# A ConvNeXt-V2 block on one core: x turned by DMA transposes while loading, the convolution as 32x32 tiles, one chunk of three evacuated by VectorE

## The chip, the core and the metric

The kernel runs on one core of a Trainium2 chip. The core has TensorE (PE, with its weight loads listed apart as PEld), VectorE (DVE), ScalarE (ACT), GpSimd (POOL), SyncE (SP, which here only issues DMAs) and 16 DMA engines. The metric is the device time of one execution in microseconds; lower is better.

## The reference, cut to what matters

```python
# x: (1, 512, 512, 96) bf16, dw: (3, 3, 96), w1: (96, 384), w2: (384, 96)
out = sum over i, j of  xp[:, i:i+H, j:j+W, :] * dw[i, j]     # depthwise 3x3, zero padding of 1
h = layernorm(out, over channels, eps=1e-5)
h = gelu(h @ w1)                                              # tanh form, 384 channels
gx = sqrt(sum of h*h over all pixels + 1e-6)                  # one number per channel
nx = gx / (mean of gx over channels + 1e-6)
h = grn_gamma * (h * nx) + grn_beta + h
return x + h @ w2
```

The sum of squares over all 512 x 512 pixels divides the kernel into two passes: no output can be made before every pixel has been through the Gelu.

## The kernel before, in words

**Blocks.** The image is cut into 128 blocks of four rows (GR = 4), 2,048 pixels each. A pixel's 96 channels are handled as three chunks of 32. The tile that comes out of the convolution has 128 partitions = 4 groups x 32 channels and, for each of the three chunks, 512 columns of pixels.

**First pass, slot by slot.** A loop over slots `s` writes all engines' work in one fixed order (the wrapper InOrder keeps the program's order on each engine, and for that reason nearly all instructions have the line of the wrapper, L35). In a slot of the steady stage stand together: the load of x for block s + 4 (`load_x`, on SP), the convolution of block s (`conv_taps`, three bursts of matmuls, `conv(0)` to `conv(2)`, and then `evac`), the layer norm of the blocks before (sums by matmuls with `rowsel`, 1/std on GpSimd, broadcast by way of DRAM into `rbc`, product `yn` on GpSimd), the writing of `yn` to DRAM and reading back as `ynT` with channels on the partitions, and for a block some slots back the first matrix and the Gelu (`mlp_units`: units of one or two PSUM banks, 12 banks in all; `unit(0, 2)` is the first, with the matmuls `PS<-ynT,w1p` and the Gelu `g<-PS`). Sums of squares of `g` come partly from BN_STATS on VectorE (`entry`, called by `squares(0)` to `squares(2)` for the first two quads of a block and by `squares_rest` for the others) and partly from matmuls of `g` with itself (`gram_next`). The order of a steady slot is:

```python
conv(0); unit(0, 2); unit(2, 1); squares(0)
conv(1, False); spread_out()
turn_x(s + 3)
unit(3, 1); unit(4, 2); squares(1); gram_next(1)
unit(6, 1); squares(2); unit(7, 1)
stage_turn(k)              # one slot in four: VectorE turns 1/std
conv(2); evac(); gram_next(1)
unit(8, 2); unit(10, 1); stage_stats(b2); unit(11, 1); squares_rest(2)
```

A `pe.drain()` follows the bursts where `fence` is true. In the steady slots the convolution always accumulates into the same three PSUM banks, `Y3`, so burst 0 of a block must wait until `evac` has read the block before.

**x, before.** `load_x` brings four rows as 128 partitions of 16 pixels, with one pixel of overlap at each side (18 pixels, 3,456 bytes per partition), into one of four `xin` buffers. `turn_x` turns it on VectorE in 32x32 blocks with two instructions per block (the first 64 channels as pairs of 32-bit words) into a ring of five `xT` tiles, where the partitions are 4 rows x 32 channels. A matmul of the convolution reads 64 partitions, that is two rows, and writes 32, one output row, so that up to two vertical taps are one matmul with the weights `Wq`: 8 tiles of the array (2 x 4), three shifts dx, three chunks, 72 matmuls per block, 24 in each burst. A row outside of the image is read from `zrow`, a tile of zeros.

**evac, before.** ScalarE copies all three banks to `y_bf` (128x1536) in bf16.

**The last 14 blocks** pass the first matrix after the last convolution (`mlp_tail`), and **the second pass** multiplies by `W2s`, adds x and the bias (`xb`, GpSimd) on VectorE (`o_sb`) and stores; parts of `g` are kept or reloaded, the rest is made again from `ynT` (`gr`).

Of the kernel before, what the change touches and what calls it, by code (L numbers as in the profile page):

```python
# [8 lines left out]
ALU = mybir.AluOpType  # L9
ACTF = mybir.ActivationFunctionType  # L10
AX = mybir.AxisListType

GR = 4
# [43 lines left out]
def kernel(  # L57
# [11 lines left out]
    f32 = mybir.dt.float32  # L69
    i32 = mybir.dt.int32  # L70
    bf16 = x.dtype
# [38 lines left out]
    def chans(i):  # L110
        return slice(i, 64, 2) if i < 2 else slice(64, 96)
# [4 lines left out]
    def quad(flat_ap, t):  # L116
        return flat_ap.rearrange("p r (t g m) -> p t g r m", t=NQ, m=MB)[:, t]

    def quad_out(flat_ap):
        return flat_ap.rearrange("p (g r m) -> p g r m", r=GR, m=MB)  # L120
# [20 lines left out]
    Wq = consts.tile([128, NI, 3, GR, 32], bf16, name="Wq")  # L141
# [41 lines left out]
    SL = PXP + 2  # L183
    with ExitStack() as p1:
# [25 lines left out]
        xinpool = pc.enter_context(tc.tile_pool(name="xin", side="right", bufs=4))  # L210
        xins = {}

        def shift(h, j):
            return 1 if (h, j) == (0, GR - 1) else -1 if (h, j) == (1, 0) else 0

        def load_x(b):
            t = xinpool.tile([128, SL, C], bf16, name="xin")
            off = x.offset + b * GR * W * C
            rows = lambda p0, p1, s0, s1: (
                t[p0:p1, s0:s1, :].rearrange("p g c -> p (g c)"),  # L220
                bass.AP(x.tensor, off + (p0 * PXP - 1 + s0) * C, [[PXP * C, p1 - p0], [1, (s1 - s0) * C]]))
            if b == 0:
                pool.memset(t[0:1, 0, :], 0.0)
                parts = [(16, 128, 0, SL), (0, 16, 1, SL), (1, 16, 0, 1)]
            elif b == NBLK - 1:
                pool.memset(t[96:128, SL - 1, :], 0.0)
                parts = [(0, 112, 0, SL), (112, 128, 0, SL - 1), (112, 127, SL - 1, SL)]
            else:
                parts = [(0, 128, 0, SL)]
            for part in parts:  # L230
                o, i_ = rows(*part)
                sp.dma_start(out=o, in_=i_)
            xins[b] = t

        Wd = gpool.tile([128, NQ, NCH, QW], bf16, name="g")[:].rearrange("p t j w -> p (t j w)")[
            :, :NI * 9 * 32].rearrange("p (i k c) -> p i k c", i=NI, k=9)
# [5 lines left out]
        for b in range(min(2, NBLK)):  # L242
            load_x(b)
        act.activation(out=warm[:], in_=warm[:], func=ACTF.Gelu_apprx_tanh)
        act.activation(out=Wq[:].rearrange("p i d j c -> p (i d j c)").rearrange("p (a w) -> p a w", a=3),
                       in_=zrow[:, None, :NI * GR * 32].to_broadcast([128, 3, NI * GR * 32]), func=ACTF.Identity)
# [8 lines left out]
        xtpool = pc.enter_context(tc.tile_pool(name="xt", side="right", bufs=1))  # L255
# [6 lines left out]
        NXT = 5  # L262
        xt_ring = []
        xt_all = xtpool.tile([128, NXT, NI, SL * MB], bf16, name="xT")
        for i in range(NXT):
            xt_ring.append(xt_all[:, i])
        assert NXT * NI * SL * MB >= NQ * NCH * QW
        g_over = xt_all[:].rearrange("p x i s -> p (x i s)")[:, :NQ * NCH * QW].rearrange(
            "p (t j w) -> p t j w", t=NQ, j=NCH)
# [32 lines left out]
        def cm_unit(g, ynt, t):  # L302
            U = banks3()
            for j in range(NCH):
                pe.matmul(quad_out(U[:, j, :]), lhsT=w1p[:, j * 128:(j + 1) * 128],
                          rhs=quad(ynt[:], t), start=True, stop=True)
            act.activation(out=g[:, t, :, :], in_=U, func=ACTF.Gelu_apprx_tanh)

        def px_unit(g, ynt, t):
            Uf = banks3().rearrange("p k w -> p (k w)")  # L310
            for r in range(GR):
                c = r * E
                while c < (r + 1) * E:
                    sz = min((r + 1) * E - c, W - c % W)
                    pe.matmul(Uf[:, c:c + sz], lhsT=ynt[:, r, t * 128:t * 128 + 128],
                              rhs=w1p[:, c - r * E:c - r * E + sz], start=True, stop=True)
                    c += sz
            act.activation(out=g[:, t, :, :].rearrange("p j w -> p (j w)"), in_=Uf, func=ACTF.Gelu_apprx_tanh)
# [9 lines left out]
        def stage_mm2(n, q):  # L328
            g, xb = grp[q]["g"], grp[q]["xb"]
            GQ = QW // 128  # L330
            o_sb = late.o.tile([128, PXP, C], bf16, name="o_sb")
            for sub in range(NSUB):
                O = out_bank()
                for gl_ in range(GPS):
                    gg = sub * GPS + gl_
                    for j in range(NCH):
# [3 lines left out]
                dve.tensor_tensor(out=o_sb[:, sub * GPS:(sub + 1) * GPS, :], in0=O,  # L340
                                   in1=xb[:, sub * GPS:(sub + 1) * GPS, :], op=ALU.add)
# [57 lines left out]
        n = 0  # L399
        for h in range(2):  # L400
            for j in range(GR):
                for q in (2 * h, 2 * h + 1):
                    a = q + GR * shift(h, j) - j + 1
                    if 0 <= a < 3:
                        n += 1
                        o, i_ = Wq[32 * q:32 * q + 32, :, :, j, :], Wd[32 * q:32 * q + 32, :, 3 * a:3 * a + 3, :]
                        if n % 2:
                            act.activation(out=o, in_=i_, func=ACTF.Identity)
                        elif n % 4:
                            dve.tensor_copy(out=o, in_=i_)  # L410
                        else:
                            pool.tensor_copy(out=o, in_=i_)

# [28 lines left out]
        def turn_x(b):  # L442
            xin = xins.pop(b)
            t = xt_ring[b % NXT]
            pairs = t[:, 0:2, :].rearrange("p i s -> p (i s)").bitcast(f32)
            dve.transpose(out=pairs.rearrange("p (g m) -> p g m", m=MB),
                          in_=xin[:, :, 0:64].bitcast(f32))
            dve.transpose(out=t[:, 2, :].rearrange("p (g m) -> p g m", m=MB), in_=xin[:, :, 64:96])

        def x_rows(b, p0, p1, i, c0, n):  # L450
            t = xt_ring[b % NXT]
            if i == 2:
                return t[p0:p1, 2, c0:c0 + n]
            return t[p0:p1, 0:2, :].rearrange("p i s -> p (i s)").rearrange(
                "p (s e) -> p s e", e=2)[:, c0:c0 + n, i]

# [6 lines left out]
        def conv_taps(b, spare):  # L463
# [6 lines left out]
            for n in range(3):  # L470
                mms.append([(h, j, (n + h) % NI, dx) for dx in (0, -1, 1) for j in range(GR) for h in range(2)])
            flat = [m for ms in mms for m in ms]
            first = {}
            last = {}
            for n, (h, j, i, dx) in enumerate(flat):
                first.setdefault((i, j), n)
                last[i, j] = n

            def burst(n, fence=True):
                k = sum(len(ms) for ms in mms[:n])  # L480
                for h, j, i, dx in mms[n]:
                    src = b + shift(h, j)
                    o0, o1 = max(0, -dx), W - max(0, dx)
                    pe.matmul(
                        Y[i][32 * j:32 * j + 32, o0:o1],
                        lhsT=Wq[64 * h:64 * h + 64, i, dx + 1, j, :],
                        rhs=x_rows(src, 64 * h, 64 * h + 64, i, MB * (1 + dx) + o0, o1 - o0)
                        if 0 <= src < NBLK else zrow[64 * h:64 * h + 64, o0:o1],
                        start=first[i, j] == k,
                        stop=last[i, j] == k,  # L490
                    )
                    k += 1
                if n < 2 and fence:
                    pe.drain()

            def evac():
                y = ypool.tile([128, NI, W], bf16, name="y_bf")
                if spare:
                    act.activation(out=y[:, 0:2, :], in_=Ua, func=ACTF.Identity)
                    act.activation(out=y[:, 2, :], in_=Ub[:, 0, :], func=ACTF.Identity)  # L500
                else:
                    act.activation(out=y[:], in_=Y3, func=ACTF.Identity)
                ybf[b] = y
# [195 lines left out]
        def mlp_units(b):  # L699
# [5 lines left out]
            def cm_mm(dst, j, t):  # L705
                pe.matmul(quad_out(dst), lhsT=w1p[:, j * 128:(j + 1) * 128], rhs=quad(yt[:], t), start=True, stop=True)

            def unit(bank, n):
# [10 lines left out]
                while c < end:  # L719
# [4 lines left out]
                    else:  # L724
# [3 lines left out]
                        col = (cm_quads(b) + t) * 128  # L728
                        pe.matmul(Uf[:, c - c0:c - c0 + sz], lhsT=yt[:, r, col:col + 128], rhs=w1p[:, e0:e0 + sz],
# [93 lines left out]
        turn_x(0)  # L823
        turn_x(1)
        turn_x(2)
        for s in range(last_slot + 1):
# [34 lines left out]
            elif not mlp:  # L861
                if s + 3 < NBLK:
                    turn_x(s + 3)
# [21 lines left out]
            else:  # L885
# [10 lines left out]
                if s + 3 < NBLK:  # L896
                    turn_x(s + 3)
# [100 lines left out]
    with p2:  # L998
        def out_part(q, o_sb, sub):
# [3 lines left out]
                    "(p g) c -> p g c", g=PXP)[:, sub * GPS:(sub + 1) * GPS],  # L1003
                in_=o_sb[:, sub * GPS:(sub + 1) * GPS])
# [47 lines left out]
```

## Time and profile before

| | |
|---|---|
| median of 3 runs | 1489.95 us (1483.42 to 1490.06) |
| profiled execution, its own time | 1482.67 us |
| its span in the trace | 1480.8 us |
| granted TensorE clock, mean | 0.994 |
| DMA | 433.08 MB, 292 GB/s on average |
| first pass with convolution | to about 885 us |
| second pass | from about 1,020 us |

In the profile a row of a group reads: line, engine, operation, out<-in by the program's names, partitions and elements with their types, number of instructions, then busy time in us, mean ns of one, and the idle time of the engine before them with what ended it. In the timeline a row reads: start in us, length in us, engine, line, operation, and how many instructions were merged into the row. In the table by windows each engine's busy us is followed by its number of instructions; then come the granted clock, the share of the 16 DMA engines that was busy, and GB/s. Ends of matmuls are modelled, so that TensorE looks fuller than it is. An instruction of ScalarE or VectorE can begin before the one ahead of it has left the pipeline, so that the distance between starts is shorter than the mean length.

### The profile page before, as it was taken

To read this page: it belongs to the slowest core of one execution; us is meant where nothing else is said; L and a number is where in the kernel's file an instruction comes from. 1 tells how busy PE (TensorE), PEld (TensorE's weight loads), DVE (VectorE), ACT (ScalarE), POOL (GpSimd) and SP (SyncE) were. 2 spreads that over 40 slices of the span, in tenths; PEclk is the share of its full clock that TensorE was granted. 3 is DMA by queue.
4 is the path that set the end of the run, shared out by engine and by line. 5 is a ranking of instruction groups with operands and counts; after the bars stand their busy time and mean duration, and the time that the engine had idled before them with its cause. 6 is when DMAs were issued, how large, how long until landed. Compare 5 with 4: busy or idle time off the path is not lost.

```text
span 1480.8 us, 54225 instructions
## 1 busy us (share of the span) xinstructions
PE 1391.3 (94%) x23125; PEld 810.4 (55%) x23125; DVE 1182.0 (80%) x2135; ACT 1414.4 (96%) x1595; POOL 1300.3 (88%) x922
## 2 busy tenths in 40 slices
PE   8888999999999999999999997789999999999998
PEld 3434444444444444444444445467777777776776
DVE  7849989999999999999999987965555555555555
ACT  7888989999999999999999999999999999999997
POOL 3459889998998999998999987569999999999997
PEclk9999999999999999999999999999999999999999
DMA  5568788788888888888888866669999999999997
GB/s 180 179 205 255 241 253 280 228 271 260 260 248 264 258 264 255 276 253 254 263 258 266 263 216 195 195 225 409 366 359 402 417 416 413 419 410 417 411 412 282
DMA packets 167768, 433.08 MB, mean 292 GB/s; under 512 B 31558, under 2 KB 81318, under 8 KB 163046
## 3 DMA queue, kind: packets, MB, share of 16 engines
q1 hardware_dynamic: 151284, 326.04, 66.3%
q0 software_dynamic: 14880, 103.43, 17.6%
q8 instruction: 181, 2.97, 0.8%
q14 instruction: 61, 0.50, 0.1%
q10 hardware_dynamic: 1362, 0.15, 0.1%
HBM read 273.30 MB, written 156.22 MB: 290 GB/s over the span
## 4 chain that ended last, share of the span: by engine, by line
PE 30%; ACT 24%; DMA 19%; POOL 13%; DVE 6%; issue 4%; SPq 4%; POOLq 0%; ACTq 0%; DVEq 0%
PE PS L35 30%; ACT g L35 16%; DMA out_dram<-o_sb 9%; POOL yn L35 6%; ACT y_bf L35 5%; POOL ysq L35 5%; SPq L35 4%; DMA yn_dram<-yn 3%; DVE bst L35 3%; DMA xin<-in_x_dram 2%; DMA rbc<-r_dram 2%; DMA ynT<-yn_dram 1%; DMA g_dram<-g 1%; DVE o_sb L35 1%; ACT xT L35 1%
## 5 line engine op out<-in xcount | busy, mean ns | idle before, releaser
L35 ACT ACTIVATE g<-PS 128x512 bf16<-128x512 f32 (+2 forms) x1062 | 727.7, 864 | 16.5 <-PE PS L35 15.6
L35 DVE BATCH_NORM_STATS2 bst<-g 128x6 f32<-128x512 bf16 x1110 | 671.3, 672 | 35.4 <-ACT g L35 34.5
L35 PE MATMUL PS<-ynT,w1p 128*128 128x512 bf16 x2181 | 609.6, 381 | 23.6 <-ACT g L35 5.4
L35 ACT ACTIVATE gr<-PS 128x1536 bf16<-128x1536 f32 x360 | 498.5, 1459 | 18.8 <-PE PS L35 13.8
L35 POOL TENSOR_TENSOR yn<-y_bf,rbc 128x1536 bf16<-128x1536 bf16 x126 | 391.3, 3108 | 77.3 <-ACT rbc L35 21.9
L35 DVE TENSOR_TENSOR o_sb<-PS,xb 128x384 bf16<-128x384 f32 x512 | 277.3, 556 | 227.0 <-PE PS L35 190.1
L324 POOL TENSOR_TENSOR xb<-xr,B2c 128x1536 f32<-128x1536 bf16 x118 | 368.1, 3133 | 4.3 <-DVE o_sb L35 2.0
L35 PE MATMUL PS<-xT,Wq 64*32 64x511 bf16 (+1 forms) x9198 | 340.5, 389 | 26.2 <-ACT y_bf L35 8.1
L35 POOL TENSOR_TENSOR ysq<-y_bf 128x1536 bf16<-128x1536 bf16 x114 | 313.6, 2752 | 12.8 <-ACT y_bf L35 12.8
L35 PEld LDWEIGHTS <-w1p 128*128 128x128 bf16 x2181 | 171.6, 98 | 222.0 <-issue 133.4
L35 PEld LDWEIGHTS <-gr 128*128 128x128 bf16 x4296 | 212.1, 98 | 68.9 <-issue 12.0
L35 PE MATMUL PS<-W2s,gr 128*128 128x96 bf16 x4224 | 223.5, 206 | 8.2 <-DVE o_sb L35 8.0
L35 PEld LDWEIGHTS <-Wq 64*32 64x32 bf16 x9216 | 111.9, 90 | 193.3 <-issue 145.9
L35 ACT ACTIVATE y_bf<-PS 128x1536 bf16<-128x1536 f32 (+2 forms) x135 | 199.4, 1482 | 17.4 <-PE PS L35 13.3
L35 DVE STREAM_TRANSPOSE xT<-xin 128x576 f32<-128x576 f32 (+1 forms) x256 | 181.4, 748 | 8.1 <-DMA xin<-in_x_dram 8.1
L35 PEld LDWEIGHTS <-g 128*128 128x128 bf16 x1704 | 104.9, 98 | 86.3 <-issue 54.3
L35 PE MATMUL PS<-w1p,ynT 128*128 128x256 bf16 (+2 forms) x822 | 125.8, 273 | 8.0 <-ACT xT L35 3.2
L35 PE MATMUL PS<-g 128*128 128x128 bf16 x1464 | 122.6, 220 | 2.9 <-DVE PS L35 2.6
L35 PEld LDWEIGHTS <-gl 128*128 128x128 bf16 x1680 | 82.8, 98 | 26.8 <-issue 5.0
L35 PE MATMUL PS<-W2s,gl 128*128 128x96 bf16 x1680 | 89.5, 206 | 3.4 <-DVE o_sb L35 3.2
L35 PEld LDWEIGHTS <-ynT 128*128 128x128 bf16 x822 | 64.1, 97 | 31.5 <-issue 13.7
L279 POOL DMA_DIRECT2D xr<-in_x_dram x115 | 63.7, 555 | 14.2 <-POOL xb L324 14.2
(105 smaller groups left out, 576.5 us busy)
## 6 DMA issues: line engine op xcount, KB each, us to landing
xin<-in_x_dram SPq DMA_DIRECT2D x126, 432.0 KB
g_dram<-g SPq DMA_DIRECT2D x105, 512.0 KB
gl<-g_dram POOLq DMA_DIRECT2D x35, 1536.0 KB, 11.3
yn_dram<-yn SPq DMA_DIRECT2D x512, 96.0 KB
ynT<-yn_dram SPq DMA_DIRECT2D x128, 384.0 KB
out_dram<-o_sb SPq DMA_DIRECT2D x127, 384.0 KB
xr<-in_x_dram POOLq DMA_DIRECT2D x123, 384.0 KB, 6.9
ynT<-yn_dram SPq DMA_DIRECT2D x85, 512.0 KB
```

The costliest lines, as they stand in the source:

```text
L35: r = f(*a, **k)
L279: pq.dma_start(out=xr[:], in_=x[0, r0:r0 + GR].rearrange("r w c -> (r w) c").rearrange("(p g) c -> p g c", g=PXP))
L324: pq.tensor_tensor(out=xb[:], in0=grp[q]["xr"][:], in1=bias[:, None, :].to_broadcast([128, PXP, C]), op=ALU.add)
```

## The change

- **Load.** `load_x` issues one DMA per block with `transpose=True`: the block's 196,608 elements, seen as 128 rows of 1,536, arrive turned, with no overlap at the sides. A partition is now one of 128 = 4 x 32 places in a run of 16 pixels x 96 channels: pixel modulo four and chunk are mixed as 3 x pixel + chunk. The ring holds six blocks in one tile `xT` (NXT = 6). `turn_x` and `xin` are gone.
- **Convolution.** The weights are `Wd`, diagonal 32x32 blocks for each chunk and tap; the copies into `Wq` are gone. A matmul reads 32 partitions and writes the 32 of one pixel of four (`sx`). A burst has one dx and runs over dy, chunk and sx. Where sx + dx leaves the four pixels, the matmul covers 384 of the 512 columns and a second one, right behind it and with the same weights, covers the remaining 124. Where the rows needed cross the end of the ring, a round is cut in two. Matmuls per block: 36 for dx = 0 and 45 for each of the other two, and more where it is cut.
- **evac.** ScalarE takes chunks 0 and 1, VectorE chunk 2.
- **Order of pixels.** With the new order of columns, `quad` is a plain slice, `quad_out` is gone, and the second pass writes and reads `o_sb` and `xb` with a step of four pixels.

```diff
 def chans(i):
-    return slice(i, 64, 2) if i < 2 else slice(64, 96)
+    return slice(32 * i, 32 * i + 32)
 def quad(flat_ap, t):
-    return flat_ap.rearrange("p r (t g m) -> p t g r m", t=NQ, m=MB)[:, t]
+    return flat_ap[:, t, :]
-Wq = consts.tile([128, NI, 3, GR, 32], bf16, name="Wq")
+Wd = consts.tile([128, NI, 9, 32], bf16, name="Wd")
...
-xinpool = pc.enter_context(tc.tile_pool(name="xin", side="right", bufs=4))
+NXT = 6
+xt = xtpool.tile([128, GR, NI, NXT * 128], bf16, name="xT")
 def load_x(b):
...
+    c = b % NXT * 128
+    sp.dma_start(out=xt[:, :, :, c:c + 128].rearrange("p k a s -> p (k a) s"),
+                 in_=x[0, b * GR:(b + 1) * GR].rearrange("r w c -> (r w c)").rearrange(
+                     "(p e) -> p e", p=128), transpose=True)
...
-    for n in range(3):
-        mms.append([(h, j, (n + h) % NI, dx) for dx in (0, -1, 1) for j in range(GR) for h in range(2)])
+    for dx in (0, -1, 1):
+        mm = []
+        for dy in (0, -1, 1):
+            runs = ...                       # rows of the ring: one run, or two where it wraps
+            for r, at_, nr in runs:
+                o = slice(r * MB, (r + nr) * MB)
+                for i in range(NI):
+                    for sx in range(GR):
+                        wrap = not 0 <= sx + dx < GR
+                        q = NI * ((sx + dx) % GR) + i
+                        ko, ki = slice(0, GR), slice(0, GR)
+                        if wrap:
+                            ko, ki = (slice(1, GR), slice(0, GR - 1)) if dx < 0 else (
+                                slice(0, GR - 1), slice(1, GR))
+                        yo = Y[i][32 * sx:32 * sx + 32, :].rearrange("p (k s) -> p k s", k=GR)
+                        xi = xt[32 * (q % 4):32 * (q % 4) + 32, :, q // 4, :]
+                        w = Wd[32 * (q % 4):32 * (q % 4) + 32, i, 3 * (dy + 1) + dx + 1, :]
+                        mm.append(((i, sx), w, yo[:, ko, o], xi[:, ki, at_:at_ + nr * MB]))
+                        if wrap:
...
+                            mm.append(...)   # the remaining columns, same weights
+        mms.append(mm)
...
 def evac():
-    act.activation(out=y[:], in_=Y3, func=ACTF.Identity)
+    act.activation(out=y[:, 0:2, :], in_=Y3[:, 0:2, :], func=ACTF.Identity)
+    dve.tensor_copy(out=y[:, 2, :], in_=Y3[:, 2, :])
...
-    turn_x(s + 3)
...
 # second pass
-dve.tensor_tensor(out=o_sb[:, sub * GPS:(sub + 1) * GPS, :], in0=O,
-                  in1=xb[:, sub * GPS:(sub + 1) * GPS, :], op=ALU.add)
+dve.tensor_tensor(out=o_sb[:, sub::NQ, :], in0=O, in1=xb[:, sub::NQ, :], op=ALU.add)
```

## The prediction

> **What bounds the kernel now.** I read the totals first, then the windows table of single blocks, then the timeline of one block, then the groups by form for durations. Over the span no engine is alone:
>
> ```profile
> PE 1391.3 (94%) x23125; PEld 810.4 (55%) x23125; DVE 1182.0 (80%) x2135; ACT 1414.4 (96%) x1595; POOL 1300.3 (88%) x922
> ```
>
> The change touches the stage in which a block is convolved while an earlier one goes through the first matrix and Gelu: 114 blocks, about 90 to 885 us. The 128 evacuations of the convolution (y_bf) follow each other there every 7.03 us. The windows table of one such block (busy us and count of PE, PEld, DVE, ACT, POOL, then clock, DMA share, GB/s):
>
> ```profile
> core 0: us, PE busy (x) PEld busy (x) DVE busy (x) ACT busy (x) POOL busy (x), PEclk, DMA share, GB/s
> 550.95:557.98 7.03, 6.78 (x120) 3.15 (x120) 7.03 (x12) 7.03 (x11) 7.03 (x3) 1.00 0.80 261
> ```
>
> Everything looks full, so busy shares don't decide. The timeline of the same block does:
>
> ```profile
> 549.36 1.58 ACT L35 ACTIVATE y_bf<-PS 128x1536 bf16<-128x1536 f32 x1
> ...
> 550.69 5.93 ACT L35 ACTIVATE g<-PS 128x1024 bf16<-128x1024 f32 x9
> ...
> 550.99 0.89 PE L35 MATMUL PS<-xT,Wq 64*32 64x512 bf16 x24
> 551.32 5.40 DVE L35 BATCH_NORM_STATS2 bst<-g 128x6 f32<-128x512 bf16 x9
> ...
> 552.00 0.82 PE L35 MATMUL PS<-ynT,w1p 128*128 128x512 bf16 x3
> ...
> 556.37 1.60 ACT L35 ACTIVATE y_bf<-PS 128x1536 bf16<-128x1536 f32 x1
> 556.64 1.42 DVE L35 STREAM_TRANSPOSE xT<-xin 128x576 f32<-128x576 f32 x2
> ...
> 558.02 0.43 PE L35 MATMUL PS<-xT,Wq 64*32 64x512 bf16 x8
> ```
>
> The convolution has one set of three PSUM banks (Y3). So there is a ring: y_bf ends (549.36 + 1.58 = 550.94), burst 0 of the next convolution starts 0.05 later, and 1.22 us after that the second matmul of unit(0,2) starts; 0.46 later ScalarE starts its Gelu, and from there ScalarE runs without a gap through six Gelus and y_bf, 5.30 us. 0.05 + 1.22 + 0.46 + 5.30 = 7.03, the period, in nearly every block. It ends again at 556.37 + 1.60 = 557.97, and TensorE starts at 558.02.
>
> What slack have the others? TensorE: I set each distance between starts against the smallest of its kind, 300 to 800 us. 17 us of excess over 71 blocks, 0.24 per block, nearly all of it before burst 0; so TensorE needs 6.79. VectorE: nine BN_STATS at 0.59 start to start, 5.3, two transposes 1.4, and small ones: nothing to spare, but not in the ring. GpSimd needs 6.5.
>
> **The change part by part.** Rows by form for the costs:
>
> ```profile
> L35 DVE TENSOR_TENSOR o_sb<-PS,xb 128x384 bf16<-128x384 f32 x512 | 277.3, 556 | 227.0 <-PE PS L35 190.1 <-DMA out_dram<-o_sb 35.4 <-POOL xb L324 0.9
> L35 ACT ACTIVATE y_bf<-PS 128x1024 bf16<-128x1024 f32 x7 | 7.2, 1022 | 7.3 <-PE PS L35 7.3
> L35 DVE TENSOR_SCALAR mom<-PS 128x128 f32<-128x128 f32 x31 | 8.5, 275 | 3.3 <-PE PS L35 3.3
> L35 DVE MEMSET PS<- 128x128 f32 x34 | 5.6, 165 | 3.4
> ```
>
> *ScalarE's evacuation* shrinks from three banks (1.57) to two: 1.02 to 1.10 at the end of a queue. ScalarE's ring: 7.03 - 1.57 + 1.10 = 6.56.
>
> *VectorE's evacuation* is new, 128x512 f32 from PSUM, which no row shows. The two rows that read PSUM give (556 - 275) / 256 = 1.10 ns a column, so 0.70; the 128x512 MEMSET of PSUM (2.44 us into the span) took 0.485, so below 0.45 is unlikely. I take 0.65, nearer the readers. Where it stands matters more: in VectorE's program it follows the block's six BN_STATS of the first two quads, and the first pair of these reads the Gelu of unit(0,2). And burst 0's ninth matmul (the first of chunk 2) waits for it. So there is a second ring: 0.05 + 1.23 + 0.46, that Gelu in full 1.08, 0.03 to VectorE (30 waits for Gelu ended so), 6 x 0.59 = 3.54, copy 0.65, 0.05 = 7.09; less 0.03 for the eight matmuls that go ahead; in one slot of four VectorE's rstd transpose (0.23) stands in between, 0.06 on average. **7.12**, with the copy's bounds 6.92 to 7.17. That is the wait that takes the place of the one removed, and it is as long.
>
> *VectorE's transposes* go: 256, 1.42 per block. They weren't in the first ring, and are not in the second. VectorE then needs 5.3 + 0.65 + about 0.15 = 6.1 per block and idles before the first pair.
>
> *The matmuls.* 72 per block (64 rows, 8 tiles at once, three rounds per burst) become 36 + 45 + 45, on 32 rows, 12 different tiles at once: again three rounds per burst. A round takes 0.23 (starts at 501.754, .987, 502.214). Weight load and matmul of free tiles start 3.4 ns apart, so 12 fill in 0.04 instead of 0.03. In bursts 1 and 2 three tiles of twelve take two matmuls per round, 384 and 124 columns, 0.25 instead of 0.23, or 0.27 if the short one waits for its 90 ns weight load. Per block +0.11 to +0.19; where the ring of six wraps (one block of three) a round is split in two, up to +0.12 more. TensorE: 6.90 to 7.10. It fits into the 0.24 that TensorE waited, so it is not in the sum, but it leaves no cover.
>
> That holds only if a tile that waits doesn't hold back the matmuls behind it. The last block shows it, where matmul 7 of each round of eight reads zrow:
>
> ```profile
> 878.34 0.41 PE L35 MATMUL PS<-xT,Wq 64*32 64x512 bf16 x6
> 878.36 0.39 PE L35 MATMUL PS<-zrow,Wq 64*32 64x512 bf16 x1
> 878.36 0.60 PE L35 MATMUL PS<-xT,Wq 64*32 64x512 bf16 x3
> 878.58 0.38 PE L35 MATMUL PS<-zrow,Wq 64*32 64x511 bf16 x1
> 878.59 0.60 PE L35 MATMUL PS<-xT,Wq 64*32 64x511 bf16 x6
> 878.80 0.38 PE L35 MATMUL PS<-zrow,Wq 64*32 64x511 bf16 x1
> ```
>
> Round 1: seventh, as written. Round 2: third. Round 3: second. Each starts when its own tile is free. The Trainium skill (TensorE: Matmul & The Clock Gate, Part 3: Packing small matmuls — row/col tiling) says that matmuls start and end strictly in program order; by that the second rival below would be the forecast. The rows speak against it, though only by some 20 ns of overtaking.
>
> *The loads.* Before, a block's 432 KB took 128 packets of 3,456 B at 172 ns, 1.37 us of 16 engines. A transposed 384 KB is in no row. Lower bound: 96 pieces of 4,096 B at 199 ns, 1.2. Upper: 12,288 writes of 32 B at the 10.6 ns of the 64 B packets, 8.1. In between, the source is read in runs of 256 B, 1,536 of them; between 64 B (10.6 ns) and 1,024 B (56) that is 20 ns, 1.9 us. I take 1.9, as the source runs are whole. The rest of the block's DMA is 0.82 x 7.03 - 1.37 = 4.4 us, so 6.3 of 7.1. It stays hidden below 2.7. The Trainium skill (DMA: Bandwidth & Descriptors, Latency and other measured facts) gives a transposing DMA 261 GB/s, an estimate of 1.5 us; the sum would be the same.
>
> SP issues as many DMAs as before (0.57 each for x; SP is busy 71%). The load of block s+4 now waits for the convolution of block s-1 instead of VectorE. Set against the trace, half of the loads were issued before that, by up to 5 us. Queued behind on SP are the reads of ynT and the writes of yn and rbc, used a slot or more later, and x itself was issued some 25 us before its use. 0 to 0.1 us per block; I take 0.
>
> *Setup and ramp.* The nine Wq copies go (2.5 us), but TensorE's fill matmuls run until 8.1 us anyway. In the ramp 1.4 us of transposes stood before yn (18.36 to 19.79), and the copy of 0.65 comes in. -6 to 0; I take -3. The second half has strided o_sb and the last block's four stores in runs of 192 B: below 1 us.
>
> **Sum.** Against the profiled execution's own time, 1482.67 (span 1480.8 plus 1.9; 0.5% under the median 1489.95 of the three runs, and like the fastest, 1483.42): 114 x (7.12 - 7.03) = +10, -3: **1490**. Its own range: 6.92 to 7.27 per block and -6 to 0, so 1464 to 1510.
>
> **The rivals.**
> - *Faster.* The copy takes 0.45 and TensorE's extra is 0.11: both rings at 6.9, (6.90 - 7.03) x 114 = -15, -3: 1465. For it: ScalarE's 6.56 and VectorE's 6.1 both leave room. Against: TensorE at 6.90 is then the floor, so no more than this.
> - *Tiles in order* (slower). If the 124-column matmul holds back the queue until its tile's 384 columns have passed, bursts 1 and 2 become chains of nine steps: 0.162 (a 384-column matmul to the next), 0.014 as between rounds, 4 starts of 3.4 ns: 0.19 each, 1.71 in place of 0.46 and at the tail a little less, +2.3 per block. TensorE needs 9.1: +236, and 14 slots without Gelu 32 more: 1750. It decides as soon as the extra is over 0.35.
> - *Transposing loads too slow* (slower). Over 2.7 us a block the 16 engines are the bound: at 3.5 the block takes 7.9, +100, 1580; at the upper bound 12.5, 2100. For it: DMA share is 0.80 already. Against: the loads are one large piece each, and far ahead.
>
> **How the numbers follow.** The second ring, 1490: 0.50. Faster, 1465: 0.20. Tiles in order: 0.10. Loads: 0.20, of which 0.12 below 1640. The range goes from 1460 to 1640 and leaves out the tiles in order and the worse loads, 0.18. About 0.5%, 7.4 us, is what a measurement here can tell from no change. The forecast straddles that: of its 0.50, 0.05 faster, 0.20 the same, 0.25 slower. Faster 0.25, same 0.20, slower 0.55.
>
> **What would show it.** Right: y_bf on ScalarE near 1.1 and on VectorE near 0.65, ScalarE idle some 0.5 us per block before the Gelu of unit(0,2), VectorE idle before its first pair, and burst 0 released by VectorE's y_bf. Wrong: convolution bursts over 1.1 us each (order), waits for xT or a DMA share near 1 (loads), or a period under 6.9, which would mean that VectorE's pairs start earlier than the ring says.

## The result, and the profile after

The changed kernel takes 1571.93 us (median of 4, 1565.07 to 1577.23), where the kernel before took 1490.0 on the same chip: 1.056 times as long, 95% interval 1.051 to 1.061. That lies in the forecast range, on the side named as likeliest, but 82 us above the time forecast. The profiled execution took 1570.23, with a span of 1568.5.

Where the time went is read from the evacuations of the convolution (y_bf), one per block. The table gives their times from the two traces; "ramp" is the start of the 18th, "steady" the 110 blocks from there to the 128th, "rest" all after that.

| us | ramp | steady | rest | mean period | median period |
|---|---|---|---|---|---|
| before | 99.1 | 784.6 | 597.1 | 7.13 | 7.04 |
| after | 121.6 | 850.8 | 596.0 | 7.74 | 7.29 |

What follows the 128th evacuation, nearly all of it the second pass, takes what it took. The first pass loses 22.5 in the ramp and 66 in the steady stage. The totals of the page (busy us, share of the span, instructions):

```profile
PE 1439.7 (92%) x31801; PEld 926.0 (59%) x31801; DVE 1102.2 (70%) x2004; ACT 1372.6 (88%) x1581; POOL 1296.5 (83%) x917
```

VectorE and ScalarE have more room, and TensorE has 8,700 pairs of weight load and matmul more. The new groups by form (busy us, mean ns | idle before them, what ended it), and the durations of SP's issue of a load (shortest, median, longest ns):

```profile
L35 PE MATMUL PS<-xT,Wd 32*32 32x384 bf16 x3360 | 253.4, 336 | 12.4 <-issue 10.8
L35 PE MATMUL PS<-xT,Wd 32*32 32x124 bf16 x2040 | 170.4, 220 | 2.5 <-issue 2.5
...
L35 ACT ACTIVATE y_bf<-PS 128x1024 bf16<-128x1024 f32 x128 | 135.9, 1062 | 55.5 <-PE PS L35 55.0 <-POOL nt L35 0.3
L35 DVE CAST y_bf<-PS 128x512 bf16<-128x512 f32 x128 | 86.0, 672 | 53.4 <-PE PS L35 53.1
```

```profile
L35 SPq DMA_TRANSPOSE xT<-in_x_dram x128: 1356/2084/3003, 0.7 to 935.3; - x128
```

An undisturbed block is a little shorter than before. The windows table (columns in its first line) and the timeline (start, length, what, idle before it) of one block:

```profile
core 0: us, PE busy (x) PEld busy (x) DVE busy (x) ACT busy (x) POOL busy (x), PEclk, DMA share, GB/s
610.98:617.90 6.92, 6.83 (x177) 3.81 (x177) 5.99 (x11) 6.66 (x11) 4.91 (x2) 1.00 0.95 226
```

```profile
610.43 0.68 DVE L35 CAST y_bf<-PS 128x512 bf16<-128x512 f32 x1
...
610.98 1.01 PE L35 MATMUL PS<-xT,Wd 32*32 32x512 bf16 x36
...
612.77 3.90 ACT L35 ACTIVATE g<-PS 128x1024 bf16<-128x1024 f32 x6 [0.26 <-ACT g L35]
612.83 0.89 PE L35 MATMUL PS<-xT,Wd 32*32 32x384 bf16 x45
...
613.83 3.66 DVE L35 BATCH_NORM_STATS2 bst<-g 128x6 f32<-128x512 bf16 x6 [0.93 <-ACT g L35]
...
616.50 1.08 ACT L35 ACTIVATE y_bf<-PS 128x1024 bf16<-128x1024 f32 x1
...
617.40 0.67 DVE L35 CAST y_bf<-PS 128x512 bf16<-128x512 f32 x1
...
617.89 0.41 PE L35 MATMUL PS<-xT,Wd 32*32 32x512 bf16 x8
```

This is the ring by way of VectorE: ScalarE idles 0.26 before the Gelu of unit(0, 2), VectorE idles 0.93 before its first pair, and the ninth matmul of the next convolution waits for VectorE's copy. From the end of one copy to the end of the next: 1.66 to the Gelu, 1.06 to the first pair, 3.57 to the copy, 0.67 the copy, 6.96. Only 47 of the 110 periods are below 7.15, though; before there were 104. What the engines wait for between 300 and 900 us (total, times, longest):

```profile
DVE bst L35 <- ACT g L35: 89.4, 78, 3.1
ACT g L35 <- PE PS L35: 36.2, 48, 2.5
POOL yn L35 <- DMA rbc<-r_dram: 35.1, 10, 4.9
PE PS L35 <- issue: 26.4, 34, 1.9
...
PE PS L35 <- DVE y_bf L35: 12.4, 8, 3.0
```

Two of these are new in kind. GpSimd waits 35 us for `rbc`, a DMA, against 6.6 before. And TensorE waits 26 us for nothing that the profile shows ("issue"); before it did not at all in that window. The DMA queues of the same 600 us (packets, MB, share of 16 engines' time), first before, then after:

```profile
q1 hardware_dynamic: 78931, 151.89, 80.9%
q8 instruction: 80, 1.31, 1.0%
```

```profile
q1 hardware_dynamic: 183274, 138.46, 99.2%
q8 instruction: 115, 1.88, 1.3%
```

Fewer bytes (a load is 384 KB instead of 432, and the 600 us hold fewer blocks), and the engines are full. The queue of instructions carries nearly half as much again in packets of 16 KB: TensorE's longer program. One of TensorE's waits, in the timeline of its instructions:

```profile
664.40 0.88 PE L35 MATMUL PS<-xT,Wd 32*32 32x384 bf16 x44
667.21 0.37 PE L35 MATMUL PS<-xT,Wd 32*32 32x512 bf16 x1 [1.94 <-issue]
```

It stops one matmul short of the end of a burst, whose inputs and banks are all there, and goes on 1.27 after the end of a packet of instructions. There are 46 such stops of over 0.4 us in the first pass, 48 us together; each ends 1.2 to 1.7 us after a packet (median 1.39, where a random moment lies 2.7 after one). The kernel before has one.

The clock differs as well. The two ramps in the windows table (columns as above), first before, then after:

```profile
0.00:99.14 99.14, 84.75 (x1833) 37.72 (x1834) 68.63 (x167) 77.62 (x91) 45.16 (x57) 0.98 0.60 180
0.00:121.63 121.63, 99.66 (x3014) 58.65 (x3015) 53.55 (x142) 67.07 (x77) 43.78 (x53) 0.83 0.71 150
```

The granted clock of TensorE is 0.98 on average in the ramp before and 0.83 after; it is at 0.5 for 3.4 and 41 us. In the steady stage it is 0.99 in both. At most, (1 - 0.83) x 121.6 = 21 us of the ramp after go to the clock (an estimate), against 2 before.

### The profile page after: what moved, and what is told of

Read it like the earlier page. It is cut to its first block, busy times and chain, and to the rows that moved or that the text cites. A ratio compares the mean times of both kernels' runs of the same rounds, so it can differ in the third digit from the quotient of the medians.

```text
span 1568.5 us, 71465 instructions
## 1 busy us (share of the span) xinstructions
PE 1439.7 (92%) x31801; PEld 926.0 (59%) x31801; DVE 1102.2 (70%) x2004; ACT 1372.6 (88%) x1581; POOL 1296.5 (83%) x917
## 5 line engine op out<-in xcount | busy, mean ns | idle before, releaser
L35 DVE BATCH_NORM_STATS2 bst<-g 128x6 f32<-128x512 bf16 x1110 | 680.7, 677 | 149.1 <-ACT g L35 147.6
L35 PE MATMUL PS<-xT,Wd 32*32 32x512 bf16 (+1 forms) x17892 | 394.5, 341 | 58.3 <-issue 33.7
L35 PEld LDWEIGHTS <-Wd 32*32 32x32 bf16 x17892 | 225.6, 90 | 235.0 <-issue 209.3
L35 ACT ACTIVATE y_bf<-PS 128x1024 bf16<-128x1024 f32 x128 | 135.9, 1062 | 55.5 <-PE PS L35 55.0
L35 DVE CAST y_bf<-PS 128x512 bf16<-128x512 f32 x128 | 86.0, 672 | 53.4 <-PE PS L35 53.1
```

What stands on the lines that cost most here:

```text
L35: r = f(*a, **k)
```

## The experiments

Theory A: the turned loads fill the DMA engines, `rbc` and `ynT` come late, and all else follows. Theory B: the load of block s + 4 waits on SP for the convolution of block s - 1, because the ring has six places, and holds up what is queued behind it. Theory C: TensorE's longer program isn't fetched in time. Theory D: the copy on VectorE passes delays on to the next convolution. All in one table; "stops" are those of TensorE as above, from 10 to 970 us; "DMA" is the sum of packet times from the 25th to the 127th evacuation over 16 engines (packets that overlap can bring it above 1); "period" is the mean from the 18th.

| | median us | ratio, 95% interval | pairs | stops, us | DMA | period |
|---|---|---|---|---|---|---|
| before | | 1 | 23,125 | 1, 1.6 | 0.82 | 7.13 |
| after | 1571.93 | 1.056 (1.051 to 1.061) | 31,801 | 46, 48.2 | 1.00 | 7.74 |
| e1_plain_load | 1533.86 | 1.036 (1.032 to 1.040) | 31,489 | 30, 30.8 | 0.87 | 7.46 |
| e2_half_load | 1526.61 | 1.033 (1.027 to 1.039) | 31,489 | 31, 28.7 | 0.92 | 7.39 |
| e3_ring8 | 1562.83 | 1.056 (1.051 to 1.062) | 30,996 | 33, 43.7 | 0.99 | 7.66 |
| e4_evac_scalar | 1562.55 | 1.055 (1.051 to 1.059) | 31,489 | 48, 49.7 | 1.00 | 7.65 |
| e5_before_split | 1542.62 | 1.044 (1.039 to 1.049) | 32,341 | 32, 32.1 | 0.80 | 7.40 |
| e6_before_extra | 1539.37 | 1.040 (1.036 to 1.045) | 23,125 | 2, 1.2 | 1.03 | 7.54 |
| e7_plain_lean | 1503.38 | 1.017 (1.013 to 1.022) | 27,460 | 6, 9.3 | 0.90 | 7.21 |
| e8_after_lean | 1546.97 | 1.041 (1.038 to 1.045) | 27,460 | 7, 8.5 | 1.00 | 7.59 |
| e9_split_one | 1489.40 | 1.004 (1.001 to 1.007) | 26,197 | 6, 8.3 | 0.83 | 7.17 |
| e10_split_extra | 1610.29 | 1.086 (1.081 to 1.092) | 32,341 | 81, 91.9 | 1.00 | 8.13 |
| e11_lean_no_load | 1493.85 | 1.005 (1.003 to 1.008) | 27,460 | 7, 8.8 | 0.67 | 7.15 |
| e12_short_aggr | 1475.35 | 0.998 (0.997 to 1.000) | 27,733 | 9, 9.2 | 0.67 | 7.00 |

Each ratio is to the kernel before on the same chip (1476.94 to 1490.0). Pairs are those that the trace recorded, of which about one in a hundred is missing (after, e1, e2 and e4 have the same program for TensorE, and so have e7, e8, e11 and e12).

**The loads and the ring of six.**

e1_plain_load:

```diff
-             "(p e) -> p e", p=128), transpose=True)
+             "(p k s) -> p k s", p=128, s=128))
```

> The changed kernel with the same 128 loads into the same places, but as plain copies without turning (x is not turned, so the convolution's numbers are meaningless; all else is as in the changed kernel, the runs of 256 B too). Theory A (the 16 DMA engines are full: packets of the turned load took 31 ns on average, 3.0 us a block, beside 4.4 us of other traffic, against a block of 6.96 us): the load falls to about 1.8 us, DMA share to about 0.9, TensorE's unexplained idle time (37 us between 120 and 970 us) goes to under 10, 1485 to 1505 us. Theory B (SP: it waits for the convolution of the block before and then needs 2.1 us to issue a turned load, and rows of 1/std behind it come late): only the 1.5 us of issue go, the wait stays, 1520 to 1550. Theory C (TensorE's longer program, 31,801 pairs instead of 23,125, can't be fetched fast enough, whatever the DMA load): no change, 1560 to 1575.

e2_half_load:

```diff
-sp.dma_start(out=xt[:, :, :, c:c + 128]..., in_=..."(p e) -> p e", p=128), transpose=True)
+n = 128 if b < NXT else 64
+sp.dma_start(out=xt[:, :, :, c:c + n]..., in_=..."(p e) -> p e", p=128)[0:n], transpose=True)
```

> The changed kernel, but from block 6 on only the first 64 of the 128 rows of x are loaded and turned (half of the columns hold an older block's x, so the output differs). Same kind of packets, half as many. Theory A: 1.5 us of DMA a block, total 5.9, share 0.85, 1485 to 1505 us, TensorE's unexplained idle time under 10 us. Theory B: SP's issue falls from 2.1 to about 1.2 us, the wait stays: 1520 to 1550. Theory C: 1560 to 1575.

e3_ring8:

```diff
-NXT = 6
+NXT = 8
```

> The changed kernel with a ring of eight blocks of x instead of six, so that the load of block s+4 no longer waits for the convolution of block s-1 but for one two blocks earlier, which is long done (and rounds are cut in two in one block of four instead of one of three). Theory A: the DMA engines are as full as before, 1555 to 1575. Theory B: SP is no longer held up (it waited 133 us for TensorE between 300 and 900 us), 1490 to 1520, most of the 22 us of the ramp too. Theory C: a few us less for the fewer cut rounds, 1560 to 1570.

e4_evac_scalar:

```diff
...                            # the branch for blocks in spare banks, in the same way
-act.activation(out=y[:, 0:2, :], in_=Y3[:, 0:2, :], func=ACTF.Identity)
-dve.tensor_copy(out=y[:, 2, :], in_=Y3[:, 2, :])
+act.activation(out=y[:], in_=Y3, func=ACTF.Identity)
```

> The changed kernel with the convolution evacuated by ScalarE alone, as before the change. An undisturbed block goes back from 6.96 to about 7.03 us (ScalarE's ring), +8 us. Theory A: the disturbed blocks stay, 1570 to 1585. Theory D (VectorE's copy stands behind its turning of 1/std, so a late 1/std now holds up the next convolution: 17 us of TensorE waiting for y_bf of VectorE): those 17 us go, 1555 to 1565.

The DMA queues of e1 between 300 and 900 us:

```profile
q1 hardware_dynamic: 187612, 142.56, 85.8%
q8 instruction: 119, 1.95, 1.4%
```

e1 and e2 take away 2.0 and 2.3% of 5.6: A explains some 40% of the loss, not all as it had foreseen, and with DMA engines that are no longer full most of TensorE's stops are still there. Both times (1533.86, 1526.61) lie where B had put them, 1520 to 1550, so these two runs don't decide against B. The packets of the loads show what turning costs. They have 256 bytes in e1 as in the changed kernel, and a median of 18 ns in both; but the mean is 18.5 in e1 and 31 after, because 1.6% of the turned ones take over 100 ns, 0.8 us on average, and make 41% of the time. With half of the rows (e2) the mean is 40: the slow packets belong more to each transfer than to its bytes. So a block's load takes 1.72 us of 16 engines plain and 2.94 turned.

e3 decides on B: 34 of its loads of 96 blocks (30 to 125) start before the end of the convolution of block s - 1, in the changed kernel one; SP's idle time before them falls from 15.3 to 2.4 us (300 to 900 us); and the ratio stays at 1.056. (The view of waits still puts 108 us of SP's time down to TensorE, 133 after; it names the update that came last.) B falls. e4 takes the waits for VectorE's copy away (17 us in the steady stage to 0), TensorE's stops don't fall (48.2 to 49.7), and the ratio stays (1.055): D passes on a delay that is there without it. In us, 1562.55 lies where D had foreseen it, but that forecast counted from the changed kernel's 1571.93, and the kernel before took 1478.26 on this chip in place of 1490.0; the ratios decide.

**Each suspect alone, in the kernel before.**

e5_before_split:

```diff
-pe.matmul(Y[i][32 * j:32 * j + 32, o0:o1], ...)
+for u0, u1 in ((o0, W // 2), (W // 2, o1)):
+    pe.matmul(Y[i][32 * j:32 * j + 32, u0:u1], ...)
```

> The kernel before, with each matmul of the convolution split into two of half the columns: 144 pairs of weight load and matmul a block in place of 72 (about 9,200 more in all, to about 32,300, near the changed kernel's 31,800), with the same columns streamed. Loads and all else as before, so the DMA engines stay near 0.82 busy. Theory C (TensorE's longer program is fetched too late: stalls of 0.4 to 2 us that no semaphore explains, each ending some 1.4 us after a packet of instructions): 15 to 35 us of such stalls in the first pass, where before had none, and knock-on waits; time up by 1.5 to 3.5%, 1500 to 1530. Theory A (all of the loss comes from DMA engines filled by turned loads; the stalls come only where those are full): no such stalls, and at most 0.05 to 0.1 us a block for the additional starts in the ring, so 1478 to 1490.

e6_before_extra:

```diff
+extra = consts.tile([128, 12, 64], bf16, name="extra")
...
+if b >= 4:
+    sp.dma_start(out=extra[:]..., in_=x[0, b * GR:(b + 1) * GR].rearrange("r w c -> (r w c)").rearrange(
+        "(p e) -> p e", p=128)[0:64], transpose=True)
```

> The kernel before, with one more turned load a block (64 of the 128 rows of x that the changed kernel turns, 196 KB, into a tile that nobody reads): about 1.5 us of 16 DMA engines and 1.7 us of SP a block more, TensorE's program as before. The DMA engines come to about 7.3 us a block, full. Theory A (turned loads fill the DMA engines): DMA share 0.98 to 1.0, period 7.2 to 7.5, time up by 2 to 5%; stalls of TensorE few. Theory C (TensorE's program alone): no slower than 1%, 1478 to 1493. Theory D (turned loads are only dear together with the program fetch): DMA share near 1 but the period within 1%.

e10_split_extra, both of these edits:

> The kernel before with both additions, each matmul of the convolution split in two and 64 of the 128 rows turned once more: the two suspected costs of the change without anything else of it. If they add: 1.044 and 1.040 make 1.084, about 1605. If waits for the one lie beside waits for the other, as in the changed kernel: 1.050 to 1.070, 1555 to 1585, with 20 us or more of stalls and a DMA share near 1.

Each alone is enough to be slower, e5 by more than the 1.5 to 3.5% foreseen. e5 has the loads, the arithmetic and the evacuation of before, DMA engines no busier, and gets 32 stops. Its undisturbed period (tenth percentile) is 7.00 for 6.97, so the starts of the additional matmuls are some 4 us of its 62. From its waits, 300 to 900 us:

```profile
PE PS L35 <- issue: 18.8, 32, 2.3
```

e6 has TensorE's program of before and two stops, full DMA engines, and late `rbc`; by way of GpSimd (`yn`, then `ysq`) TensorE comes to wait:

```profile
POOL yn L35 <- DMA rbc<-r_dram: 30.7, 11, 4.8
PE PS L35 <- POOL ysq L35: 30.2, 17, 3.3
```

A late `rbc` alone doesn't tell the two causes apart, though: GpSimd waits 25.7 us for it in e5 too.

Together they give 1.086, and the product of the two is 1.086: the waits for the one don't lie beside the waits for the other. That the two costs are independent doesn't follow, as the stops show. TensorE's stops in e10, in the same 600 us as those of e5 above:

```profile
PE PS L35 <- issue: 60.6, 63, 2.6
```

With the DMA engines full the same program stops 81 times in place of 32 (92 us for 32). If these are fetches, they suffer from the full engines too, but only where the program is long: e6 and e8 have full engines and hardly a stop.

**How many pairs it takes.**

e7_plain_lean has the plain loads of e1, e8_after_lean the turned ones; both:

```diff
-for r in range(GR):
-    ...                        # one run of rows, or two
+r0 = b * GR % (NXT * GR)
+runs.append([0, min(max(r0 + dy, 0), (NXT - 1) * GR) * MB, GR])
...
-            if wrap:
+            if False:
                 mm.append(...)   # the remaining columns
```

> The changed kernel with plain loads of the same bytes (not turned, so the data are not the reference's) and without the 124-column matmuls and the split rounds: always 108 pairs of weight load and matmul a block in place of 126 to about 150 (the pixels that wrap to the next line are left out). Theory C: stalls fall by more than half from the 22 us of the run with plain loads alone, first pass 15 to 30 us shorter than there, 1500 to 1520. If the number of pairs does not matter (the rest of the loss lies in the ring or in the ramp): within 8 us of 1534. If the ring sets the time once all else is free, 128 blocks of 6.96: about 1470 to 1480.

> The changed kernel with its turned loads, without the 124-column matmuls and the split rounds: always 108 pairs a block (the pixels that wrap to the next group are left out). Two separate causes (A the DMA engines, C the program of TensorE): DMA share stays 0.98 to 1.0, stalls of TensorE after the ramp under 5 us as with plain loads and 108 pairs, and the time falls from 1.056 by the 0.019 that the pairs were worth with plain loads: 1.032 to 1.045, 1528 to 1547. If the full DMA engines delay the program fetch as well (one cause): 15 us or more of stalls, 1.045 to 1.055.

e9_split_one:

```diff
-for u0, u1 in ((o0, W // 2), (W // 2, o1)):
+for u0, u1 in ((o0, W // 2), (W // 2, o1)) if n == 1 else ((o0, o1),):
```

> The kernel before with only the middle one of the three bursts of a block split in halves: 96 pairs a block, about 26,200 in all, between 23,125 (one stall) and 27,460 (six, all in the ramp). Fetch with a limit (stalls begin where the program is used up faster than it comes): at most 6 stalls, time up by 0 to 1.2%, 1480 to 1498. Cost in proportion to the additional pairs (a third of the 62 us of all three bursts): about 10 stalls, 1498 to 1506.

C is borne out: with 108 pairs a block the stops fall from 30 to 6 (plain loads) and from 46 to 7 (turned), and of the few that are left at most one lies behind the ramp. The price isn't in proportion: 26,197 pairs cost 0.4%, 32,341 cost 4.4%. With DMA engines that aren't full, a packet of instructions came every 7.5 us before (300 to 900 us), 6.2 in e9 (three stops there), 5.8 in e7 (none), 5.0 in e1 and 4.8 in e5 (stops all the way). So, by these averages, the limit lies between one packet in 5.8 and one in 5.0 us; e9's three stops at 6.2, with its additional pairs in one burst of three, say that it also counts how they are spread. e8's DMA engines stay full (the queue's line of the same 600 us), and it is at 1.041:

```profile
q1 hardware_dynamic: 184901, 139.56, 100.0%
```

That is near e6's 1.040, though not all of it is the engines (below), and the other theory of that run, stops of 15 us and more, falls. Part of the price of full engines can be the clock: the steady stages of e6 and e8 have 0.97 of it, that of e7 0.99, that of e12 1.00. No run here separates the two. That the stops are fetches rests on two things, their place after a packet and the number of pairs; the profile names no cause for them. e8 against the changed kernel gives the additional matmuls 1.4%; e1 against e7 gives them 1.9%.

**What is left without the loads.**

e11_lean_no_load, beside the edits of e7:

```diff
 def load_x(b):
+    if b >= NXT:
+        return
```

> As the run with plain loads and 108 pairs, and x is loaded for the first six blocks only (later blocks read what lies in the ring): what the convolution and the divided evacuation give when nothing of the loads is left. If what is left of that run (1.017) is the loads: DMA share about 0.67, mean period 6.95 to 7.05, 1470 to 1485. If it is TensorE's program or the ring itself: 1495 to 1505.

e12_short_aggr, beside those of e11:

```diff
-dve.bn_aggr(out=mv[:, j, k, :], in_=bst[:, j, :GROUPS[k], :].rearrange("p a s -> p (a s)"))
+dve.bn_aggr(out=mv[:, j, k, :], in_=bst[:, j, :1, :].rearrange("p a s -> p (a s)"))
```

> As the run without loads and with 108 pairs a block, and each BATCH_NORM_AGGREGATE takes one of 32 entries in place of all, so that three of them last some 0.6 us in place of 2.76 (the sums for the scaling of the second matrix are left out by that). In that run all ten of them in the steady part stand in a long period (8.6 to 10 us in place of 6.97): VectorE's copy of y_bf queues behind them, and the next convolution behind the copy. If they are what eats the shorter ring: those periods fall to 7.0 to 7.2, mean period 6.97 to 7.03, first pass 12 to 18 us shorter than in that run, 1474 to 1484, ratio 0.991 to 0.998. If the long periods have another cause (the rstd chain on GpSimd, the program): 1490 to 1497 as there.

e11 lies between its two forecasts, above what was foreseen if the loads were all, though it gains 1.2% on e7. The median period is 6.97, yet the kernel isn't faster than before. Ten of its twelve periods above 7.3 have a BATCH_NORM_AGGREGATE just ahead, which closes a group of 32 entries; of before's six, one has. Its timeline of VectorE:

```profile
621.95 2.76 DVE L35 BATCH_NORM_AGGREGATE mv<-bst 128x2 f32<-128x192 f32 x3
624.63 3.59 DVE L35 BATCH_NORM_STATS2 bst<-g 128x6 f32<-128x512 bf16 x6
628.14 0.67 DVE L35 CAST y_bf<-PS 128x512 bf16<-128x512 f32 x1
```

The 2.76 push the six BN_STATS and the copy back, and the ring closes 1.6 later (8.58). Before, VectorE stood outside of the ring, and the same three instructions cost nothing there: nine of the ten periods behind them take 7.0 to 7.1. e12 shortens them, by form:

```profile
L35 DVE BATCH_NORM_AGGREGATE mv<-bst 128x2 f32<-128x6 f32 x39 | 3.8, 154 | 0.0
```

The long periods go (4 above 7.3 in place of 12), the steady stage falls by 16.5 us, and the ratio is 0.998, at the edge of what was foreseen.

So the 5.6% come apart, each step from two rows of the table and, by their intervals, good to some 0.3 to 0.6 points: the new convolution and the divided evacuation without any loads -0.2 (e12, within noise of nothing), the aggregates +0.7 (e11), plain loads in runs of 256 bytes, against none at all, +1.2 (e7), turning them +2.4 (e8), the pairs beyond 108 +1.4 (after). In another order the steps differ: the pairs are 1.9 with plain loads (e1 to e7). No version here beats the kernel before clear of noise, and e12, which leaves out most loads and most of the aggregates' work, suggests that little was to be had: TensorE is busy 588 of these 600 us, by the profile's modelled ends of matmuls.

```profile
300.00:900.00 600.00, 588.46 (x13390) 323.74 (x13388) 525.21 (x942) 575.15 (x846) 568.29 (x435) 1.00 0.67 204
```

## Why the prediction was right or wrong

The range held, in part by luck. The slowdown was forecast from a second ring of 7.12 us against 7.03; undisturbed, that ring takes 6.96, and 7.10 in one slot of four (e12), so by itself it makes the kernel no slower. What made it slower were the loads, in the forecast a rival of 0.20, and two costs that it put at nothing, the aggregates and TensorE's additional pairs.

**Right: the ring and the bursts.** The ring by VectorE's copy is there: ScalarE's part 1.06 (1.02 to 1.10 foreseen), the copy 0.67 (0.65), and burst 0 released by it. The period is 6.96, not 7.12: the sum counted the 0.05 at the copy's end twice; the way to the Gelu took 1.66, not 1.71, and the Gelu and its hand-over to VectorE 1.06, not 1.11; BN_STATS and copy took 0.05 more. The other 0.06 were for VectorE's rstd transpose, which isn't in this block; where it is, the period is 0.13 longer (e12), 0.03 on average. The bursts of 45 take 0.89 as those of 24 did, so tiles don't wait in order, and that rival is false. There the Trainium skill's rule of strict program order (TensorE: Matmul & The Clock Gate, Part 3) would have made nine steps of each burst; the trace shows three: twelve starts, then the three short ones, three times over. The second pass was forecast to change by less than 1 us; all that follows the 128th evacuation took 1.1 less.

**Wrong: "small ones" on VectorE.** The aggregates, 2.76 per 10.6 blocks, were among them and counted at nothing, as they had been before. Once VectorE is in the ring, what it does there counts: +0.7%, shown by e12. With them the mean period of e11 is 7.15, which is why 7.12 looks right and is not.

**Mis-sized: the loads.** 1.9 us of 16 engines were foreseen for 1,536 runs of 256 bytes at 20 ns; it is 2.94. The run's price was good (median 18), but the slow ones in a turned transfer lift the mean to 31. The Trainium skill (DMA: Bandwidth & Descriptors, Latency and other measured facts) gives 261 GB/s for a transposing DMA, measured on one kernel, an estimate of 1.5; the trace has half of that rate. The rest of the block's DMA is 4.78, not 4.4 (its 4,096-byte packets went from 198 to 215 ns on average). 2.94 + 4.78 = 7.72 is the mean period, but at a share of 1.00 it can't be otherwise; that the loads cost time is shown by e8 against e7 and by e6, not by this sum. So the third rival, loads too slow beyond 2.7, is a good part of what happened: 2.4% by turning, of 5.6. Its price, (2.94 + 4.4 - 7.03) x 114 = 35 us, is not far from the 41.7 by which the steady stages of e7 and e8 differ. The sign of it in the text, a DMA share near 1, was there; waits for xT were not, and GpSimd's for `rbc` were.

**Missing: TensorE's program.** The sum had each pair at 3.4 ns of start and nothing for bringing it. That is the 1.4% between e8 and the changed kernel and, since its starts are some 4 us of 62, most of e5's 4.4%. The ramp, forecast at -3 and measured at +22.5, has 13 us of the stops before 121.6 us; e12, with 8 us of stops in its ramp, loses 11 there. The sum has no term for the clock either, and the ramp's is at 0.83 (e12 0.92, e5 0.86; before 0.98), worth 21 us at most. Stops and clock could together be more than was lost; how the 22.5 divide between them, and what lowers the clock, stays open. The Trainium skill (Runtime: NRT & Kernel Launch, Instruction fetch mechanics) calls the crossing of a 16 KB boundary mostly hidden. If the stops are fetches, the kernel before agrees from 10 to 970 us, with one stop for 125 packets of instructions; the changed kernel has 46 for 187, and e10 81 for 179.

**Mis-sized without harm: SP.** "As many DMAs as before" holds, but a turned load holds SP for 2.1 us on average where a plain one held it for 0.57, and SP is busy 0.85 of the stage in place of 0.69. e1 (0.72 each) and e2 (1.69) have the same time within their intervals, and e3 shows that the hold by the ring costs nothing that can be measured here.

## What to carry to other kernels

Before taking an engine into the ring that sets the period, list everything on that engine's queue, the rare instructions too: what was free beside the ring can cost inside it (here some 1.6 of the 2.76 us of each group of aggregates). Count instructions as a resource of their own: smaller tiles of the array take no longer per burst, but a straight-line program of short matmuls has to be brought in, and here that cost was small up to 108 pairs a block and large at some 140. And read the granted clock of each stage: up to 21 us of the ramp went to it here, and the forecast had no term for it. Where the DMA engines are at 0.8, price a new load by the mean of its packets and not by the median, and add it to the sum of all others before calling it hidden.

## What the runs showed of the hardware

- Packets of a turned load: median 18 ns, as the plain ones of 256 bytes, but 1.6% over 100 ns (0.8 us on average); plain 0.01%. Half of the rows gives a mean of 40 ns, not 31.
- TensorE goes on 1.2 to 1.7 us (1.0 to 1.9 over all runs) after the end of a 16 KB packet of instructions that takes 1.1 us; in no run do two such packets start less than 3.3 us apart. Why the fetch is not further ahead, when a packet is needed only every 5 us, isn't shown by these runs.
- Two thirds and more of the stops (33 of 46 after, 27 of 32 in e5) lie inside the bursts of the convolution, where the pairs are densest.
- 12 tiles of 32x32 with 45 matmuls take 0.89 us, as 8 tiles of 64x32 with 24.
- In the stretches of e6 with a granted clock of 0.5, neighbouring matmuls of the first matrix (128x512) start 410 ns apart on average, and 224 at full clock.
